# Clustered attention, an MLP and a soft mixture of experts in one kernel: the MLP stage's softmax in groups of two tiles, a fourth PSUM bank, tokens two chunks sooner

## The chip, the cores and the metric

The kernel runs on one core of a Trainium2 chip, as one program. The metric is the device time of one execution in microseconds. A core has five engines that run side by side, each through its own list of instructions in order, and that wait for one another by semaphores: TensorE (PE in the profile, with its weight loads as PEld), VectorE (DVE), ScalarE (ACT), GpSimd (POOL) and SyncE (SP), which here only issues DMA transfers. TensorE writes to PSUM, a small memory of eight banks; each bank holds 512 float32 numbers in each of 128 partitions.

## The reference

Three layers follow one another. Only the second and the logits and sums of the third lie in the stage that is changed.

```python
def _moe_ref(x, w_in, w_out):          # x: 3072 tokens x 512, from the attention
    h = x @ w_in                       # 512 -> 2048
    g = h * np.cos(h)
    return g @ w_out                   # 2048 -> 512

def _moe2_ref(x, phi, w1, w2):         # 32 slots, 8 experts
    logits = x @ phi
    d = np.exp(logits - logits.max(0)) ; d /= d.sum(0) + 1e-09     # softmax over all tokens
    slot_input = d.T @ x
    ...                                # each expert: relu(slot_input @ w1) @ w2
    c = np.exp(logits - logits.max(1)) ; c /= c.sum(1) + 1e-09     # softmax over the 32 slots
    return c @ slot_out
```

## The kernel before

The program has three stages: the attention, the MLP, and a tail with the experts and the output.

**The MLP stage** takes the 3072 tokens in 24 tiles of 128 tokens, and each tile in four chunks of 512 hidden columns: 96 chunks, numbered c, with c // 4 the tile for the first 22 tiles. (The last two tiles are taken together, chunk by chunk.) The loop at L1016 issues one chunk per pass, and every engine gets its instructions in the order in which the passes write them. No scheduler moves them. In pass c stand:

- `hchunk(c)`, L128: 12 matmuls of 512 columns that add up h in one PSUM bank with the tag "s". There are three such banks, so h of chunk c + 3 uses the bank of chunk c again.
- `post2(c-2)`, L855: ScalarE takes a sine, ScalarE or VectorE squares it, and VectorE writes g = h cos h (L865, called gg). This is the last reader of h, so it frees the bank.
- `post1(c-1)`, L139: a copy on ScalarE (L142), two operations on VectorE (L143, L144).
- `gtr(c-3)`, L867: four transposes of g on TensorE; `gev(c-4)`, L875: their copy out of PSUM into a buffer gts, of which there are four.
- In each fourth pass `logit` (L883): 4 matmuls per chunk, 16 in all, form the slot logits of a whole tile in the bank m1 (the trace shows each float32 matmul twice). wphi already holds w_out times phi, so that the logits come from g directly.
- Then the tile's online softmax, in steps that hang on one another over several passes. `soft1` (L901) copies the logits, `soft2` (L908) adds them up on TensorE into the bank m2 (lf, lt) and takes maxima on VectorE (L920 to L924). `softx` and `softe` (L928, L940) take exponentials on ScalarE; before them and behind them ScalarE loads another function table. `soft3` to `soft5` sum, transpose the exponentials (dt, bank v), multiply them with g (accp, bank v) and add the product to acc (L990).

A token tile comes in three steps: `xload` (L92, three DMAs on SP's queue into the one buffer xr), `xprep` (L103: GpSimd multiplies at L106, VectorE makes a mask at L108, GpSimd adds at L110) and `xprep2` (L112: VectorE casts the high part at L117, GpSimd makes the low part at L118, which is the last reader of xr). The table `xsched` (L1003) puts them in passes 4t - 5, 4t - 3 and 4t - 2 for tile t.

**The tail** multiplies with 32 MB of expert weights. They come in 16 pieces of 2 MB. Pieces 0 to 3 are loaded in passes 28, 36, 44 and 52 into buffers of the pool wk (six buffers; two hold w_out). Piece 4 follows when the last chunk with the first quarter of w_in is done (pass 89), as it takes that weight's place; pieces 5 to 7 follow in passes 91, 93 and 95, and the rest in the tail.

Of the kernel before, what the change touches and what calls it, by code (L numbers as in the profile page):

```python
# [8 lines left out]
F32 = mybir.dt.float32  # L9
# [10 lines left out]
P = 128  # L20
# [6 lines left out]
def clustered_attention_then_soft_moe(  # L27
# [16 lines left out]
    DM, DF = w_in.shape  # L44
    NS = phi.shape[1]
# [44 lines left out]
    R = {}  # L90
# [31 lines left out]
    order = [(t, f) for t in range(NT - GRP) for f in range(NF)]  # L122
    order += [(t, f) for f in range(NF) for t in range(NT - GRP, NT)]
    NC_ = len(order)
    groups = [[t] for t in range(NT - GRP)] + [list(range(NT - GRP, NT))]
    at_last = {max(c for c in range(NC_) if order[c][0] in ts): ts for ts in groups}

    def hchunk(c):  # L128
        t, f = order[c]
        hi, lo = R["xs", t]  # L130
        h = psum.tile([P, 512], F32, tag="s", name=f"h{c}", bufs=3)
        n = 0
        for d in range(DT):
            for x, w in ((hi, 0), (hi, 1), (lo, 0)):
                PE.matmul(h, lhsT=x[:, d, :], rhs=wc[f][:, w, d, :], start=(n == 0), stop=(n == 3 * DT - 1))  # L135
                n += 1
        R["h", c] = h
# [706 lines left out]
    with ExitStack() as m:  # L844
# [3 lines left out]
        R["m"] = m0  # L848
        zero = phis.rearrange("p a s -> p (a s)").bitcast(BF16)
        POOL.memset(zero, 0.0)  # L850
        wo = [wk.tile([P, 8, DM], F32, tag="wk", name=f"wo{x}") for x in range(2)]
        gs_stack = ExitStack()
        gsp = gs_stack.enter_context(tc.tile_pool(name="gsp", bufs=4))

        def post2(c):  # L855
            t, f = order[c]
            h, r = R.pop(("h", c)), R.pop(("r", c))
            if f == 0:
                R["g", t] = ggp.tile([P, DF], F32, tag="gg", name=f"gg{t}")
            ACT.activation(out=r, in_=r, func=AF.Sin, scale=0.5)  # L860
            if c == NC_ - 2 or (c % 4 in (0, 2)):
                ACT.activation(out=r, in_=r, func=AF.Square)  # L862
            else:
                (POOL if c == NC_ - 3 else DVE).tensor_tensor(out=r, in0=r, in1=r, op=ALU.mult)  # L864
            DVE.scalar_tensor_tensor(out=R["g", t][:, f * 512:(f + 1) * 512], in0=r, scalar=0.5, in1=h, op0=ALU.subtract, op1=ALU.mult)  # L865
# [7 lines left out]
            R["gp", c] = g  # L873

        def gev(c, eng=None):  # L875
            s = gsp.tile([P, 512], F32, tag="gts", name=f"gts{c}")
            if eng is DVE:
                DVE.tensor_copy(s, R.pop(("gp", c)))
            else:
                ACT.activation(out=s, in_=R.pop(("gp", c)), func=AF.Copy)  # L880
            R["gt", c] = s

        def logit(c):  # L883
            t, f = order[c]
            s = R.pop(("gt", c))
            if f == 0:
                if t < NT - GRP:
                    R["lp", t] = psum.tile([P, P], F32, tag="m1", name=f"lp{t}")
                elif t == NT - GRP:
                    R["lpg"] = psum.tile([P, GRP, P], F32, tag="m1", name="lpg")  # L890
                    for j in range(4):
                        PE.matmul(R["lpg"][32 * j:32 * j + 32].rearrange("p a b -> p (a b)"), lhsT=zero[:, 0:32], rhs=zero,
                                  start=True, stop=False)
                if t >= NT - GRP:
                    R["lp", t] = R["lpg"][:, t - NT + GRP, :]
            lp = R["lp", t]
            for j in range(4):
                PE.matmul(lp[32 * j:32 * j + 32, :], lhsT=wphi[:, 4 * f + j, :], rhs=s[:, j * P:(j + 1) * P],  # L898
                          start=(f == 0 and t < NT - GRP), stop=(f == NF - 1 and (t < NT - GRP or t == NT - 1)))
# [8 lines left out]
        def soft2(ts):  # L908
            n = len(ts)
            lps = R["lps"]  # L910
            lfb = psum.tile([P, n * (P + NS)], F32, tag="m2", name=f"lf{ts[0]}")
            lf = lfb[:, 0:n * P]
            lt = lfb[:, n * P:].rearrange("p (a b) -> p a b", a=n)
            PE.matmul(lf, lhsT=gflat, rhs=lps, start=True, stop=True)
            for y in range(n):
                PE.matmul(lt[:, y, :], lhsT=lps[:, y * P:(y + 1) * P], rhs=gmat[:, 0, :], start=True, stop=True)
            mn = mp.tile([P, 1], F32, tag="mrun", name=f"mrun{ts[0]}")
            ng = mp.tile([P, 1], F32, tag="ng", name=f"ng{ts[0]}")
            rn = mp.tile([P, n], F32, tag="rn", name=f"rn{ts[0]}")
            DVE.tensor_reduce(out=mn, in_=lf, op=ALU.max, axis=AX.X)  # L920
            DVE.tensor_tensor(out=mn, in0=mn, in1=R["m"], op=ALU.max)
            DVE.tensor_scalar(out=ng, in0=mn, scalar1=-1.0, scalar2=None, op0=ALU.mult)
            DVE.tensor_reduce(out=rn, in_=lt, op=ALU.max, axis=AX.X)
            DVE.tensor_scalar(out=rn, in0=rn, scalar1=-1.0, scalar2=None, op0=ALU.mult)  # L924
            R["soft2"] = lf, lt, R["m"], ng, rn
            R["m"] = mn
# [47 lines left out]
        def soft4(ts):  # L974
            n = len(ts)
            cr, dts = R["dts"]
            ap = psum.tile([P, 512], F32, tag="v", name=f"accp{ts[0]}")
            for y, t in enumerate(ts):
                g = R.pop(("g", t))
                for j in range(4):  # L980
                    PE.matmul(ap[32 * j:32 * j + 32, :], lhsT=dts[:, y * P + 32 * j:y * P + 32 * j + 32],  # L981
                              rhs=g[:, j * 512:(j + 1) * 512], start=(y == 0), stop=(y == n - 1))
            R["ap"] = cr, ap
# [18 lines left out]

        xsched = {}  # L1003
        for t in range(1, NT):
            c0 = min(4 * t - 5, NF * (NT - GRP) - 4 - 3 * (NT - 1 - t))
            for fn, dc in ((xload, 0), (xprep, 2), (xprep2, 3)):
                if c0 + dc >= 2:
                    xsched.setdefault(c0 + dc, []).append((fn, t))
# [6 lines left out]

        for c in range(2, NC_):  # L1016
            hchunk(c)
            post2(c - 2)
            if c - 1 < NC_ - 1:
                post1(c - 1)  # L1020
            if c >= 4:
                gev(c - 4)
            if c - 6 in at_last:
                softx(at_last[c - 6])
                softe(at_last[c - 6])
            if c - 7 in at_last and at_last[c - 7][0] != NT - GRP - 1:
                soft3(at_last[c - 7])
            for fn, t in xsched.get(c, ()):
                fn(t)
            late_c = at_last.get(c - 7)  # L1030
            if late_c and late_c[0] == NT - GRP - 2:
                soft3b(late_c)
            if c >= 3:
                gtr(c - 3)
            if c % 4 == 3:
                for x in range(max(c - 7, 0), c - 3):
                    logit(x)
            if c - 4 in at_last:
                soft1(at_last[c - 4])
            if c - 5 in at_last:  # L1040
                soft2(at_last[c - 5])
            if late_c and late_c[0] < NT - GRP - 2:
                soft3b(late_c)
            elif late_c and late_c[0] == NT - GRP - 2:
                soft4(late_c)
                soft5(late_c)
            if at_last.get(c - 6) == [NT - GRP - 1]:
                soft3b(at_last[c - 6])
                soft3(at_last[c - 6])
            elif at_last.get(c - 7) == [NT - GRP - 1]:  # L1050
                soft4(at_last[c - 7])
            late_c = at_last.get(c - 8)
            if late_c and late_c[0] < NT - GRP - 2:
                soft4(late_c)
                soft5(late_c)
            if c == 5:
                recip(B - 1)
                while late:
                    tick()
            if c in (12, 20):  # L1060
                x = (c - 12) // 8
                for y in range(2):
                    SP.dma_start(out=wo[x][:, 4 * y:4 * y + 4], in_=wod.rearrange("(f y p) d -> y p f d", f=4, p=P)[2 * x + y])
            if c in (28, 36, 44, 52):
                load_piece((c - 28) // 8, wk, "wk")
            if c == NC_ - 6:
                w8 = R["mxa"].tile([P, 1024], F32, tag="xr", name="w8b", bufs=1)
                load_part(8, 2, w8)
            if NC_ - GRP * NF <= c and (NC_ - 1 - c) % GRP == 0:
                if c == NC_ - 1:  # L1070
                    w8 = ggp.tile([P, 2, 1024], F32, tag="gg", name="w8a")
                    for e in range(2):
                        load_part(8, e, w8[:, e])
                load_piece(NF - 1 - (NC_ - 1 - c) // GRP + 4, wbig, "wbig")
# [248 lines left out]
```

## Time and profile before

| | us |
|---|---|
| three runs | 905.78, 907.83, 907.93 (median 907.83) |
| the profiled execution, its own time | 906.36 |
| its span in the profile | 904.6 |

| engine | busy us | share of the span |
|---|---|---|
| PE | 873.0 | 97% |
| PEld (weight loads) | 623.2 | 69% |
| DVE | 702.2 | 78% |
| ACT | 666.4 | 74% |
| POOL | 453.0 | 50% |

The MLP stage's first h matmul starts at 452.7 us and its last one starts at 833.3 us. Before it lies the attention, behind it the tail. In a row of the timeline, the first number is the start in microseconds from the span's start, the second the time that the merged instructions took; then come engine, source line, operation, what is written from what, the shapes and the count. A bracket at the end tells how long the engine sat idle before it and which instruction ended that. Matmuls overlap, so the step from one row's start to the next one's tells more of TensorE's pace than a row's length.

### The profile page before, as it was taken

To read this page: it belongs to the slowest core of one execution; us is meant where nothing else is said; L and a number is where in the kernel's file an instruction comes from. 1 tells how busy PE (TensorE), PEld (TensorE's weight loads), DVE (VectorE), ACT (ScalarE), POOL (GpSimd) and SP (SyncE) were. 2 spreads that over 40 slices of the span, in tenths; PEclk is the share of its full clock that TensorE was granted. 3 is DMA by queue.
4 is the path that set the end of the run, shared out by engine and by line. 5 is a ranking of instruction groups with operands and counts; after the bars stand their busy time and mean duration, and the time that the engine had idled before them with its cause. 6 is when DMAs were issued, how large, how long until landed. Compare 5 with 4: busy or idle time off the path is not lost.

```text
span 904.6 us, 16891 instructions
## 1 busy us (share of the span) xinstructions
PE 873.0 (97%) x5991; PEld 623.2 (69%) x5991; DVE 702.2 (78%) x1495; ACT 666.4 (74%) x1364; POOL 453.0 (50%) x344
## 2 busy tenths in 40 slices
PE   7899999999999999999999999999999999999996
PEld 4666767676667676666567777777777777777443
DVE  7899898988899889999967777777777767776203
ACT  6688888898888898886556676777767777676323
POOL 3478888888788887889832222222322222310000
PEclk9999999999999999999999999999999999999998
DMA  7676766765766675644310431333040101128998
GB/s 165 143 180 165 192 164 160 181 164 145 190 159 170 171 183 142 176 132 142 111 34 26 140 117 48 117 128 126 27 141 24 47 25 40 32 76 301 392 351 301
DMA packets 127816, 129.51 MB, mean 143 GB/s; under 512 B 57851, under 2 KB 105205, under 8 KB 127733
## 3 DMA queue, kind: packets, MB, share of 16 engines
q1 hardware_dynamic: 126020, 128.02, 49.2%
q8 instruction: 47, 0.77, 0.4%
q10 hardware_dynamic: 1712, 0.43, 0.2%
q14 instruction: 37, 0.29, 0.1%
HBM read 86.18 MB, written 16.97 MB: 114 GB/s over the span
## 4 chain that ended last, share of the span: by engine, by line
PE 33%; DVE 5%; ACT 5%; issue 4%; DMA 2%; SPq 2%; POOL 1%; POOLq 0%; ACTq 0%
PE h L135 21%; PE gt L872 3%; PE lp L898 2%; SPq L836 2%; PE accp L981 2%; DMA wh<-in_moe_w_dram 2%; DVE gg L865 1%; PE fo L1257 1%; ACT L860 1%; ACT kk L860 1%; ACT L936 1%; DVE kk L144 1%; ACT kk L862 1%; PE o L453 1%; DVE kk L864 1%
## 5 line engine op out<-in xcount | busy, mean ns | idle before, releaser
L471 POOL TENSOR_TENSOR ps<-ps,a 128x768 f32<-128x768 f32 x124 | 233.9, 1886 | 60.4 <-ACT a L444 55.4
L135 PE MATMUL h<-wc,xhi 128*128 128x512 f32 x768 | 251.5, 408 | 5.3 <-DVE gg L865 5.2
L396 DVE TENSOR_REDUCE mc<-sm 128x1 f32<-128x384 f32 x384 | 200.2, 553 | 33.7 <-PE sm L394 30.3
L444 ACT ACTIVATE a<-s 128x384 f32<-128x384 f32 x384 | 179.4, 494 | 19.4 <-PE s L441 13.7
L135 PEld LDWEIGHTS h<-wc,xhi 128*128 128x128 f32 x768 | 137.7, 189 | 55.0 <-DVE kk L144 16.8
L135 PE MATMUL h<-wc,xlo 128*128 128x512 f32 x384 | 152.5, 397 | 0.0
L440 PE MATMUL s<-st 96*128 96x384 f32 (+1 forms) x384 | 142.9, 372 | 1.3 <-ACT a L444 0.2
L453 PE MATMUL o<-a,vt 128*64 128x384 f32 x768 | 136.0, 497 | 0.0
L441 PE MATMUL s<-st 128*128 128x384 f32 x384 | 131.1, 341 | 0.0
L394 PE MATMUL sm<-st 96*128 96x384 f32 x384 | 123.2, 356 | 4.8 <-DVE mc L396 3.4
L865 DVE SCALAR_TENSOR_TENSOR gg<-kk,h 128x512 f32<-128x512 f32 x96 | 66.0, 688 | 51.7 <-ACT kk L862 48.3
L453 PEld LDWEIGHTS o<-a,vt 128*64 128x64 f32 x768 | 53.0, 138 | 64.9 <-issue 60.7
L860 ACT ACTIVATE kk<-kk 128x512 f32<-128x512 f32 x96 | 60.7, 632 | 40.1 <-DVE kk L144 39.8
L440 PEld LDWEIGHTS s<-st 96*128 96x128 f32 (+1 forms) x384 | 73.1, 190 | 23.9 <-issue 17.5
L135 PEld LDWEIGHTS h<-wc,xlo 128*128 128x128 f32 x384 | 72.5, 189 | 17.6
L106 POOL TENSOR_TENSOR xr<-xr 128x512 f32<-128x512 f32 x24 | 31.2, 1301 | 105.6 <-DMA xr<-recs 105.6
L394 PEld LDWEIGHTS sm<-st 96*128 96x128 f32 x384 | 72.0, 191 | 13.8 <-DVE mc L396 6.9
L441 PEld LDWEIGHTS s<-st 128*128 128x128 f32 x384 | 73.0, 190 | 0.0
L110 POOL TENSOR_TENSOR xr<-xr 128x512 f32<-128x512 f32 x24 | 31.3, 1306 | 80.3 <-DVE xr L108 76.0
L118 POOL TENSOR_TENSOR xlo<-xr,xhi 128x512 fp32r<-128x512 f32 x24 | 36.5, 1521 | 67.3 <-DVE xhi L117 67.3
L144 DVE SCALAR_TENSOR_TENSOR kk<-kk,h 128x512 f32<-128x512 f32 x96 | 66.0, 688 | 3.3
L468 POOL TENSOR_TENSOR ps<-a,a 128x768 f32<-128x768 f32 x31 | 56.8, 1833 | 6.9 <-ACT a L444 4.9
(230 smaller groups left out, 1495.4 us busy)
## 6 DMA issues: line engine op xcount, KB each, us to landing
st<-st SPq DMA_DIRECT2D x128, 192.0 KB
w<-in_moe_w_dram SPq DMA_DIRECT2D x8, 2048.0 KB
wh<-in_moe_w_dram SPq DMA_DIRECT2D x23, 512.0 KB
w<-in_moe_w_out_dram SPq DMA_DIRECT2D x16, 512.0 KB
w<-in_moe_w_in_dram SPq DMA_DIRECT2D x16, 512.0 KB
qt<-in_q_dram SPq DMA_DIRECT2D x32, 192.0 KB
vt<-in_v_dram SPq DMA_DIRECT2D x16, 384.0 KB
xnum<-num SPq DMA_DIRECT2D x32, 192.0 KB
```

The lines of the kernel that those rows point to most:

```text
L135: PE.matmul(h, lhsT=x[:, d, :], rhs=wc[f][:, w, d, :], start=(n == 0), stop=(n == 3 * DT - 1))
L144: DVE.scalar_tensor_tensor(out=a, in0=a, scalar=-TWO_PI, in1=h, op0=ALU.mult, op1=ALU.add)
L394: PE.matmul(m[:, 0:QW], lhsT=st[0:96, Q1 + h, qt * P:(qt + 1) * P], rhs=st[0:96, K1 + h, half * QW:(half + 1) * QW], start=True, stop=True)
L396: DVE.tensor_reduce(out=s["mc"][:, col:col + 1], in_=m[:, 0:QW], op=ALU.max, axis=AX.X)
L440: PE.matmul(x[:, 0:QW], lhsT=st[0:n, K1 + h, ks], rhs=st[0:n, Q1 + h, qs], start=True, stop=False)
L441: PE.matmul(x[:, 0:QW], lhsT=st[:, K2 + h, ks], rhs=st[:, Q2 + h, qs], start=False, stop=True)
L444: ACT.activation(out=T[i][u][:, h, :], in_=x[:, 0:QW], func=AF.Exp, scale=scale)
L453: PE.matmul(s["o"][64 * h:64 * h + 64, 0:QW], lhsT=s["v"][:, h, kt, :], rhs=t[:, h, :], start=(kt == 0), stop=(kt == KT - 1))
L468: (DVE if i == NPAIR - 1 and qc else POOL).tensor_tensor(out=ps, in0=s[u - 1], in1=t, op=ALU.add)
L471: (DVE if i == NPAIR - 1 and qc else POOL).tensor_tensor(out=ps, in0=ps, in1=t, op=ALU.add)
L860: ACT.activation(out=r, in_=r, func=AF.Sin, scale=0.5)
L865: DVE.scalar_tensor_tensor(out=R["g", t][:, f * 512:(f + 1) * 512], in0=r, scalar=0.5, in1=h, op0=ALU.subtract, op1=ALU.mult)
```

## The change

The softmax of tiles 0 to 19 is done for two tiles at a time. The logits of eight chunks (32 matmuls) run in one pass, c % 8 == 3; the two tiles share one logit bank, one copy, one sum, one set of maxima, one table load to the exponentials and one back. The products with g follow 12 passes behind the pair's last chunk instead of 8 behind the tile's. Tiles 20 to 23 stay as they are.

Since g of five tiles must now be kept, two more slots (gx) and the eight gts slots (gtx) are taken from the pool wk. The sum lf moves from bank m2 to m1, which it shares with the logits, and each fourth chunk's h goes to m2. Token loads, preparation and split stand two passes sooner (4t - 7, 4t - 5, 4t - 4; tile 2 one pass). Weight pieces 2 and 3 take the buffers of gtx and gx, and so move from passes 44 and 52 to passes 84 and 88.

```diff
-    groups = [[t] for t in range(NT - GRP)] + [list(range(NT - GRP, NT))]
+    NPR = 20
+    groups = [[t, t + 1] for t in range(0, NPR, 2)] + [[t] for t in range(NPR, NT - GRP)] + [list(range(NT - GRP, NT))]
...
     def hchunk(c):
         t, f = order[c]
         hi, lo = R["xs", t]
-        h = psum.tile([P, 512], F32, tag="s", name=f"h{c}", bufs=3)
+        if c % 4 == 3:
+            h = psum.tile([P, 512], F32, tag="m2", name=f"h{c}")
+        else:
+            h = psum.tile([P, 512], F32, tag="s", name=f"h{c}", bufs=3)
...
+        gtx = wk.tile([P, 8, 512], F32, tag="wk", name="gtx")
+        gx = wk.tile([P, 2, DF], F32, tag="wk", name="gx")
...
-                R["g", t] = ggp.tile([P, DF], F32, tag="gg", name=f"gg{t}")
+                if t < NPR and t % 5 > 2:
+                    R["g", t] = gx[:, t % 5 - 3]
+                else:
+                    R["g", t] = ggp.tile([P, DF], F32, tag="gg", name=f"gg{t}")
...
-            s = gsp.tile([P, 512], F32, tag="gts", name=f"gts{c}")
+            s = gtx[:, c % 8] if c < NF * NPR else gsp.tile([P, 512], F32, tag="gts", name=f"gts{c}")
...
-                if t < NT - GRP:
+                if t < NPR:
+                    if t % 2 == 0:
+                        R["lpg"] = psum.tile([P, 2, P], F32, tag="m1", name=f"lp{t}")
+                    R["lp", t] = R["lpg"][:, t % 2, :]
+                elif t < NT - GRP:
                     R["lp", t] = psum.tile([P, P], F32, tag="m1", name=f"lp{t}")
...
-            lfb = psum.tile([P, n * (P + NS)], F32, tag="m2", name=f"lf{ts[0]}")
+            lfb = psum.tile([P, n * (P + NS)], F32, tag="m1", name=f"lf{ts[0]}")
...
-            c0 = min(4 * t - 5, NF * (NT - GRP) - 4 - 3 * (NT - 1 - t))
+            c0 = min(max(4 * t - 7, 3 * t - 4), NF * (NT - GRP) - 4 - 3 * (NT - 1 - t))
...
-            if c % 4 == 3:
-                for x in range(max(c - 7, 0), c - 3):
+            if c < NF * (NPR + 1):
+                if c % 8 == 3:
+                    for x in range(max(c - 11, 0), c - 3):
+                        logit(x)
+            elif c % 4 == 3:
+                for x in range(c - 7, c - 3):
                     logit(x)
...
+            late_c = at_last.get(c - 12)
+            if late_c and late_c[0] < NPR - 2:
+                soft4(late_c)
+                soft5(late_c)
             late_c = at_last.get(c - 8)
-            if late_c and late_c[0] < NT - GRP - 2:
+            if late_c and NPR - 2 <= late_c[0] < NT - GRP - 2:
                 soft4(late_c)
                 soft5(late_c)
...
-            if c in (28, 36, 44, 52):
-                load_piece((c - 28) // 8, wk, "wk")
+            if c in (28, 36, 84, 88):
+                load_piece((28, 36, 84, 88).index(c), wk, "wk")
```

Three places show how the instructions move. The first is TensorE's list around the logits of tile 10 (lp10); gt are transposes, accp the products with g, lf the sums, x4 counts matmuls of one form. Before, and then in the changed kernel:

```order
L872 MATMUL gt44_8239<-ident_68,gg11_8186 128x128 x4
L898 MATMUL lp10_8244<-gts40_8112,wphi_78 32x128 x4
L898 MATMUL lp10_8244<-gts41_8152,wphi_78 32x128 x4
L898 MATMUL lp10_8244<-gts42_8194,wphi_78 32x128 x4
L898 MATMUL lp10_8244<-gts43_8233,wphi_78 32x128 x4
L981 MATMUL accp9_8263<-gg9_7834,dts9_8211 32x512 x4
...
L872 MATMUL gt45_8291<-ident_68,gg11_8186 128x128 x4
L914 MATMUL lf10_8296<-lps10_8261,gmat_74 128x128
L916 MATMUL lf10_8296<-gmat_74,lps10_8261 128x32
```

```order
L881 MATMUL gt48_8172<-ident_68,gg12_8131 128x128 x4
L911 MATMUL lp10_8177<-gtx_6305,wphi_78 32x128 x32
L994 MATMUL accp8_8212<-gx_6306,dts8_8024 32x512 x8
...
L881 MATMUL gt49_8247<-ident_68,gg12_8131 128x128 x4
L927 MATMUL lf10_8252<-lps10_8210,gmat_74 128x256
L929 MATMUL lf10_8252<-gmat_74,lps10_8210 128x32 x2
```

Two tiles' logits and two tiles' products now stand in one block, the sum is one matmul of 256 columns, and it comes four chunks later (behind gt49 instead of gt45).

The second place is VectorE's list around the maxima of tile 10 (mrun10, ng10, rn10); the cast xhi belongs to a later tile. Before, and then in the changed kernel:

```order
L117 CAST xhi12_8200<-xr12_8058 128x512
L864 TENSOR_TENSOR kk45_8190<-kk45_8190 128x512
L865 SCALAR_TENSOR_TENSOR gg11_8186<-kk45_8190,h45_8132 128x512
L143 TENSOR_SCALAR kk46_8229<-kk46_8229 128x512
L144 SCALAR_TENSOR_TENSOR kk46_8229<-kk46_8229,h46_8173 128x512
L990 SCALAR_TENSOR_TENSOR acc_6297<-acc_6297,corr9_8154,accp9_8263 128x512
...
L144 SCALAR_TENSOR_TENSOR kk47_8285<-kk47_8285,h47_8213 128x512
L920 TENSOR_REDUCE mrun10_8299<-lf10_8296 128x1
L921 TENSOR_TENSOR mrun10_8299<-mrun10_8299,mrun9_8122 128x1
L922 TENSOR_SCALAR ng10_8300<-mrun10_8299 128x1
```

```order
L1003 SCALAR_TENSOR_TENSOR acc_6297<-acc_6297,corr8_7971,accp8_8212 128x512
L874 SCALAR_TENSOR_TENSOR gg12_8131<-kk50_8161,h50_8118 128x512
L147 TENSOR_SCALAR kk51_8238<-kk51_8238 128x512
L148 SCALAR_TENSOR_TENSOR kk51_8238<-kk51_8238,h51_8145 128x512
L117 CAST xhi14_8243<-xr14_8109 128x512
L933 TENSOR_REDUCE mrun10_8256<-lf10_8252 128x1
L934 TENSOR_TENSOR mrun10_8256<-mrun10_8256,mrun8_7942 128x1
L935 TENSOR_SCALAR ng10_8257<-mrun10_8256 128x1
```

The cast, and with it the GpSimd operation that follows it, has moved to a place right ahead of the maxima.

The third place is SP's list behind the last token loads (w2 to w7 are weight pieces). Before, and then in the changed kernel:

```order
L97 DMA xr23_9878<-xnum3_83 128x4x128
L100 DMA xr23_9878<-recs3_91 64x4x128 x2
L841 DMA w4_10104<-in_moe2_w1_dram 128x4x1024
L836 DMA w8b_10148<-in_moe2_w2_dram 128x1024
L841 DMA w5_10197<-in_moe2_w1_dram 128x4x1024
```

```order
L97 DMA xr23_9500<-xnum3_83 128x4x128
L100 DMA xr23_9500<-recs3_91 64x4x128 x2
L845 DMA w2_9521<-in_moe2_w1_dram 128x4x1024
L845 DMA w3_9701<-in_moe2_w1_dram 128x4x1024
L845 DMA w4_9738<-in_moe2_w1_dram 128x4x1024
L840 DMA w8b_9782<-in_moe2_w2_dram 128x1024
L845 DMA w5_9831<-in_moe2_w1_dram 128x4x1024
```

Pieces 2 and 3 now stand between the last token load and piece 4.

## Rows read from the trace of the kernel before

**Rows 1.** Windows, mid stage: stretch, length, five engines busy (PE first), clock, DMA share, GB/s.

```profile
526.30:651.70 125.40, 125.38 (x875) 97.73 (x873) 94.26 (x233) 93.45 (x185) 33.43 (x24) 1.00 0.31 102
```

**Rows 2.** Waits view of PE and PEld, 452 to 836 us.

```profile
PE h L135 <- DVE gg L865: 5.2, 7, 2.0
...
PEld h L135 <- DVE gg L865: 7.6, 9, 2.3
```

**Rows 3.** Timeline and windows around the longest of these waits.

```profile
772.95 0.88 DVE L108 TENSOR_SCALAR xr<-xr,vm 128x128 f32<-128x128 f32 x4 [2.52 <-POOL xr L106]
...
777.11 1.22 PE L135 MATMUL h<-wc,xhi 128*128 128x512 f32 x2 [2.04 <-DVE gg L865]
...
778.00:779.00 1.00, 1.00 (x4) 0.71 (x4) 0.45 (x2) 1.00 (x1) 0.40 (x1) 0.50 0.00 0
...
781.57 0.60 PE L872 MATMUL gt<-ident,gg 128*128 128x128 f32 x4
```

**Rows 4.** Timeline of PE, one tile (four chunks) without a wait.

```profile
620.40 0.73 PE L135 MATMUL h<-wc,xhi 128*128 128x512 f32 x2
...
623.30 0.60 PE L872 MATMUL gt<-ident,gg 128*128 128x128 f32 x4
...
625.70 0.73 PE L135 MATMUL h<-wc,xhi 128*128 128x512 f32 x2
...
628.60 0.60 PE L872 MATMUL gt<-ident,gg 128*128 128x128 f32 x4
629.03 0.39 PE L914 MATMUL lf<-lps,gmat 128*128 128x128 f32 x2
629.26 0.31 PE L916 MATMUL lf<-gmat,lps 128*128 128x32 f32 x2
629.40 0.71 PE L135 MATMUL h<-wc,xhi 128*128 128x512 f32 x2
...
632.28 0.60 PE L872 MATMUL gt<-ident,gg 128*128 128x128 f32 x4
632.63 0.72 PE L135 MATMUL h<-wc,xhi 128*128 128x512 f32 x2
...
636.04 0.74 PE L135 MATMUL h<-wc,xhi 128*128 128x512 f32 x2
```

**Rows 5.** Timeline, a tile's softmax on ACT, then the DVE and PE instructions behind it.

```profile
756.98 1.28 ACT L936 ACT_TABLE_LOAD   x1 [0.51 <-DVE rn L923]
...
758.81 0.28 ACT L944 ACTIVATE e<-lf,rn 128x32 f32<-128x32 f32 x1
...
759.20 1.28 ACT L860 ACT_TABLE_LOAD   x1
...
761.83 0.69 DVE L865 SCALAR_TENSOR_TENSOR gg<-kk,h 128x512 f32<-128x512 f32 x1 [1.57 <-ACT kk L862]
...
762.57 0.73 PE L135 MATMUL h<-wc,xhi 128*128 128x512 f32 x2
```

**Rows 6.** Timeline, the small maximum at L921 alone, and beside a GpSimd operation.

```profile
756.45 0.16 DVE L921 TENSOR_TENSOR mrun<-mrun,mrun 128x1 f32<-128x1 f32 x1
...
773.97 1.27 POOL L110 TENSOR_TENSOR xr<-xr 128x512 f32<-128x512 f32 x1 [1.05 <-DVE xr L108]
774.06 1.20 DVE L921 TENSOR_TENSOR mrun<-mrun,mrun 128x1 f32<-128x1 f32 x1
```

**Rows 7.** DMA issues of the page; timeline and windows at the stage's end.

```profile
w<-in_moe_w_dram SPq DMA_DIRECT2D x8, 2048.0 KB
...
809.76 0.38 SPq L841 DMA_DIRECT2D w<-in_moe_w_dram  x1
...
825.00:830.00 5.00, 5.00 (x29) 3.81 (x32) 2.57 (x8) 4.85 (x12) 0.00 (x0) 1.00 0.55 186
830.00:835.00 5.00, 5.00 (x60) 3.57 (x52) 3.11 (x7) 2.80 (x6) 1.04 (x1) 1.00 1.02 360
```

**Rows 8.** Timeline of POOL, the first token operation behind a 2 MB piece.

```profile
568.80 1.29 POOL L106 TENSOR_TENSOR xr<-xr 128x512 f32<-128x512 f32 x1 [7.24 <-DMA xr<-recs]
```

## The prediction

> **What bounds the kernel now.** I read the busy lines of the page first: TensorE has 97% of the span. The windows view tells whether that is real work. In the middle of the MLP stage TensorE is busy in 125.38 of 125.40 us, at the full clock of 2.4 GHz (column PEclk 1.00), and no other engine comes near [rows 1]. So in this stage time is saved in two ways only: TensorE waits less, or it gets less to do.
>
> The waits view of the stage comes next. TensorE waits for one thing: the operation gg at L865, which frees an h bank. The weight loads, which are what TensorE does first in a chunk, waited 7.6 us for it, 9 times, at most 2.3 us; the matmuls behind them show 5.2 us in 7 waits [rows 2]. I count the weight loads' figure, since a chunk can't begin without them.
>
> The timeline at the longest wait shows a second cost. VectorE stood 2.52 us for the tokens of a tile whose load came late, gg slid back, and TensorE stood still. From then its granted clock was 0.50, its lower level of 1.2 GHz, and that chunk took 781.57 - 777.11 = 4.46 us [rows 3] where an undisturbed one takes 623.30 - 620.40 = 2.90 us [rows 4]. So 1.56 us more belong to this wait.
>
> Last I read how near the other tiles are to waiting. After a tile's softmax on ScalarE, gg starts at 761.83, ends 0.69 later at 762.52, and the h chunk that needs its bank starts at 762.57 [rows 5]. The slack is 0.05 us. Nothing may be added to that path with three banks.
>
> **The change part by part.** The sum is made against the profiled execution's own 906.36 us (span 904.6, the 1.8 around it left alone). The median of the runs is 1.5 us above that; the runs spread over 2.15 us, more than the differences that I expect between single tiles, and I forecast on the scale of the profile.
>
> *Fourth bank.* h of chunk c + 4, not c + 3, now needs gg of chunk c. The transposes of chunk c need it too, and they stand behind h of chunk c + 3. So the relief is one chunk of h matmuls, 2.90 us [rows 4], and the longest wait was 2.3 [rows 2]. All nine go, if nothing else comes later: -7.6. What is late next is looked at below. I leave one ninth in place, +0.8, for the first tiles, whose tokens can't come sooner: tile 2's load waits for tile 1's split in the one buffer xr. Ends: nothing left, or half left (+3.8).
>
> *Tokens two passes sooner.* The same three GpSimd operations, five VectorE ones and three DMAs per tile, two passes ahead on VectorE's and POOL's lists and on SP's queue. Each load still waits for the split before it, so in the steady tiles only the place moves. The longest wait is different: there a cap put tile 21's load into the pass of tile 20's split. Now the load stands one pass behind it. With the wait goes the low clock: -1.56. Tile 23 keeps such a pass.
>
> *Less for TensorE.* Two tiles have the same number of logit matmuls and products, and as these stream back to back (2.40 us from 623.30 to 625.70 [rows 4]) I count no gain. The sum lf is another matter. A chunk with it takes 629.40 - 628.60 = 0.80 us from its transposes to the next h, one without 632.63 - 632.28 = 0.35: lf and lt cost 0.45 per tile. For a pair, the second lt costs 629.40 - 629.26 = 0.14, and 128 more columns in two matmuls cost 2 x 128/512 of an h matmul, itself about 2.90/12 = 0.24: 0.12. So 0.71 instead of 0.90, 0.19 per pair, 10 pairs: -1.9. Ends: 0, and -4.5 if the second tile's share were free.
>
> *Less for ScalarE and VectorE.* Half the softmax steps of 20 tiles go, among them 20 table loads of 1.28 us [rows 5]. Neither bounds the stage, so this counts as slack and not as time.
>
> *The pair's own path.* It is longer than a tile's, and with 0.05 us of slack this is what could turn the sign. Logits of eight chunks and two products stand ahead on TensorE itself, so they delay both sides alike. From the sum on, the other side grows. The second e adds 759.20 - 758.81 = 0.39 [rows 5]. At the most everything between the table loads doubles (758.26 to 759.20: 0.94), and the maxima too (756.45 to 756.98: 0.53 [rows 5, 6]): 1.47. Then the collision. Alone the maximum at L921 takes 0.16; beside a GpSimd addition it took 1.20 [rows 6]. In the changed list the cast stands right ahead of the maxima and GpSimd's subtraction follows the cast, so each pair may meet it: 1.04 more. Together 0.4 to 2.5 us against 0.05 + 2.90 = 2.95. I take it as covered: 0. With three banks the same pairs would wait.
>
> The Trainium skill (SBUF — State Buffer, Who interferes with whom) says that a VectorE operation with two inputs in SBUF and a GpSimd operation that reads SBUF share a port, and that the second blocks until the first ends. The trace agrees: 1.20 against 0.16. By that rule the collision is no accident but comes with every pair; by the rows it costs TensorE nothing while the bank's relief holds.
>
> *Weight pieces 2 and 3 in passes 84 and 88.* The tail is where the transfers bound: from 830 us on the DMA engines are full (share 1.02, 360 GB/s). Before that they are not: 0.55 at 186 GB/s from 825 to 830, which is 338 GB/s while busy, and 2.25 us idle [rows 7]. A piece is 2.1 MB [rows 7], 6.2 us at that rate. Piece 2 goes out behind tile 23's load, about five chunks ahead of piece 4, and has the engines to itself. Piece 3 waits for the products of tiles 18 and 19 in pass 87. On SP, piece 4 and all behind it stand behind this wait. From those products to the end of chunk 89, which releases piece 4 (809.76 before [rows 7]), lie two chunks: 2 x (2.90 + 0.35) + 0.45 = 6.95 us. So piece 3 is through when piece 4 may start, and a spill up to 2.25 us falls into the idle time. I take 0; ends 0 and 12.4, both pieces in full.
>
> Sum: 906.36 - 7.6 - 1.56 - 1.9 + 0.8 = 896.1. I say 896.
>
> **The rivals.**
>
> *Waits stay in part.* Piece 2 stands right behind tile 23's load. The one row like that shows GpSimd waiting 7.24 us for its tokens [rows 8], and tile 23 has its split and load so close that VectorE may again stand, as it did for 2.52. If that gives one long wait and its low clock back, 2.3 + 1.56, the time is 900. Against it: the fourth bank covers 2.9.
> The Trainium skill (DMA: Bandwidth & Descriptors, Issuing engines are not separate DMA queues) says that transfers run on the same 16 engines and interleave. The 7.24 us agree with that.
>
> *One piece spills into the tail.* If piece 3 comes a piece late, the full tail shifts by 6.2: 902. For it: the tail has no idle time after 830. Against it: the 6.95 us.
>
> *Gain and loss cancel.* Both pieces spill (+12.4, 908.5), or the collision isn't covered and each pair waits 1.04 (+10.4, 906.5).
>
> *Slower: the pair's path outgrows the bank.* Place: gg of the chunks behind a pair's table loads. VectorE also stands at L1003 for two products, with gg of the next chunk behind it, and then has the cast, the collision and the maxima in a row. If the path is 2.3 us over, as long as the worst wait before, ten pairs cost 23: 919. It decides from 1.0 us per pair, where it eats the gain of 10.3. For it speaks the 0.05 us; against it that even the upper bound of 2.5 lies under 2.95.
>
> **How the numbers follow.** Forecast 896: 0.64. Waits stay in part, 900: 0.16. One piece spills, 902: 0.08. Gain and loss cancel, 906.5 to 908.5: 0.07. Slower, 919: 0.05. What a measurement can tell from no change is 0.3%, 2.7 us around 907.83. So faster 0.88, the same 0.07, slower 0.05. The range reaches from 891 (no wait left, lf almost free: 906.36 - 9.16 - 4.5 = 892.7, less the 1.5 us by which the runs lie on either side) to 904, which takes in the second and third case. About 0.13 lies outside.
>
> **What would show it.** Right: in the profile after, the waits view has hardly a wait of PE or PEld for gg; the granted clock is 1.00 throughout the stage; two tiles take about 31.1 us (2 x 15.64 - 0.19; a tile is 636.04 - 620.40 [rows 4]); from the first h to the last the stage is some 10 us shorter; from piece 4's issue to the end it is as long as before, 904.6 - 809.76 = 94.8 us [rows 7]. Wrong: a wait of h or gt for gg in every second tile at the same chunk means the pair's path; a tail longer than 95 us with the DMA share at 1.0 from piece 3 on means the pieces; VectorE waiting at the mask of tile 23 means the late load.

## The result, and the profile after

The changed kernel takes 897.39 us (median of four runs, 896.75 to 897.91) against 906.81 us for the kernel before (905.68 to 907.93). The ratio is 0.9887, 95% interval 0.9872 to 0.9902: 1.1% faster. The profiled execution took 897.9 us, and its span is 896.2 us against 904.6.

The stage is where the time went. From the start of the first h to the start of the last, TensorE took 833.31 - 452.72 = 380.59 us before and 824.69 - 454.21 = 370.47 us now: 10.1 us less. The span is only 8.4 us shorter, because in this execution the first h starts 1.5 us later. That lies in the attention, which is untouched; in a second profile of the same kernel the first h starts at 452.80, the stage is again 370.47 and the span 894.9.

In mid stage TensorE still never rests, at the full clock (windows view of the changed kernel, columns as in [rows 1]):

```profile
526.30:651.70 125.40, 125.40 (x914) 99.14 (x916) 90.61 (x201) 80.93 (x160) 32.79 (x25) 1.00 0.26 84
```

ScalarE has 12.5 us less to do there, but TensorE was the bound in [rows 1], and it still is. What it does in one pair shows in its timeline, start us, duration, operation:

```profile
554.67 0.71 PE L139 MATMUL h<-wc,xhi 128*128 128x512 f32 x2
...
557.56 0.60 PE L881 MATMUL gt<-ident,gg 128*128 128x128 f32 x4
558.09 1.95 PE L911 MATMUL lp<-gtx,wphi 128*32 128x128 f32 x64
559.86 1.04 PE L994 MATMUL accp<-gg,dts 128*32 128x512 f32 x8
560.72 1.04 PE L994 MATMUL accp<-gx,dts 128*32 128x512 f32 x8
561.69 0.73 PE L139 MATMUL h<-wc,xhi 128*128 128x512 f32 x2
...
564.60 0.60 PE L881 MATMUL gt<-ident,gg 128*128 128x128 f32 x4
565.03 0.60 PE L927 MATMUL lf<-lps,gmat 128*128 128x256 f32 x2
565.46 0.53 PE L929 MATMUL lf<-gmat,lps 128*128 128x32 f32 x4
565.83 0.72 PE L139 MATMUL h<-wc,xhi 128*128 128x512 f32 x2
...
585.49 0.71 PE L139 MATMUL h<-wc,xhi 128*128 128x512 f32 x2
```

The pair takes 585.49 - 554.67 = 30.82 us; two tiles took 2 x 15.64 = 31.28 [rows 4]. One block of 64 logit matmuls and 16 products, from transposes to h, is 561.69 - 557.56 = 4.13. Before there were two blocks of 625.70 - 623.30 = 2.40 [rows 4], so 0.67 is gone; part of it comes back, since a chunk that had such a block now has a plain gap of about 0.35 from its transposes to h. The sum lf is no cheaper than before: 565.83 - 564.60 = 1.23, less that gap 0.88, where two tiles paid 0.90.

The waits view of the stage shows what is left where [rows 2] had 5.2 and 7.6 us:

```profile
PE gt L881 <- DVE gg L874: 1.8, 2, 1.5
PE gt L881 <- ACT gts L889: 1.3, 1, 1.3
...
PE gt L881 <- ACT gtx L889: 0.2, 1, 0.2
```

No h waits for gg any more. The 1.8 us are waits of the transposes, while the third tile's h is running. Chunk by chunk, against the same chunk of a steady pair, the first five tiles lose 0.2 to 1.6 us at six places, 3.4 us in all. The timelines of POOL, DVE and PE at the worst of them answer to [rows 3]:

```profile
485.96 1.29 POOL L106 TENSOR_TENSOR xr<-xr 128x512 f32<-128x512 f32 x1 [4.63 <-DMA xr<-recs]
...
487.29 0.88 DVE L108 TENSOR_SCALAR xr<-xr,vm 128x128 f32<-128x128 f32 x4 [1.46 <-POOL xr L106]
...
491.07 1.30 POOL L118 TENSOR_TENSOR xlo<-xr,xhi 128x512 fp32r<-128x512 f32 x1 [1.49 <-DVE xhi L117]
...
491.29 1.63 DVE L873 TENSOR_TENSOR kk<-kk 128x512 f32<-128x512 f32 x1 [0.36 <-ACT kk L869]
492.95 0.69 DVE L874 SCALAR_TENSOR_TENSOR gg<-kk,h 128x512 f32<-128x512 f32 x1
...
493.79 0.63 PE L881 MATMUL gt<-ident,gg 128*128 128x128 f32 x4 [1.45 <-DVE gg L874]
```

It is tile 21's pattern in small: VectorE stands at the mask for tokens (1.46 us), then its square L873 meets GpSimd's subtraction L118 (1.63 us where the square alone takes 0.68), and gg is late. The granted clock stays at 1.00 from 484 to 500 us.

### The profile page after: what moved, and what is told of

Same layout as the page of the kernel before. It is cut to its first block, busy times and chain, and to the rows that moved or that the text cites. A ratio compares the mean times of both kernels' runs of the same rounds, so it can differ in the third digit from the quotient of the medians.

```text
span 896.2 us, 16761 instructions
## 1 busy us (share of the span) xinstructions
PE 867.8 (97%) x5971; PEld 621.9 (69%) x5971; DVE 685.5 (76%) x1405; ACT 631.3 (70%) x1294; POOL 448.2 (50%) x344
## 4 chain that ended last, share of the span: by engine, by line
PE 38%; issue 4%; DVE 3%; SPq 2%; DMA 2%; ACT 1%; POOL 1%; POOLq 0%; ACTq 0%
PE h L139 25%; PE gt L881 4%; PE lp L911 2%; PE accp L994 2%; SPq L840 2%; PE fo L1278 1%; DMA wh<-in_moe_w_dram 1%; DMA xr<-recs 1%; PE o L457 1%; PE so L1254 1%; PE lf L927 0%; DVE kk L148 0%; DVE gg L874 0%; POOL xlo L118 0%; PE lf L929 0%
## 5 line engine op out<-in xcount | busy, mean ns | idle before, releaser
L139 PE MATMUL h<-wc,xhi 128*128 128x512 f32 x768 | 248.8, 405 | 0.0
L874 DVE SCALAR_TENSOR_TENSOR gg<-kk,h 128x512 f32<-128x512 f32 x64 | 43.9, 686 | 45.4 <-ACT kk L871 42.6
L146 ACT ACTIVATE kk<-h 128x512 f32<-128x512 f32 x96 | 55.9, 582 | 1.1 <-PE h L139 1.0
```

Source lines behind the costliest of these rows:

```text
L146: ACT.activation(out=a, in_=h, func=AF.Copy, scale=1.0 / TWO_PI)
```

## The experiments

All runs are compared with the kernel before, on the same chip. The stage is counted from the first h to the last in each profile; a pair is two steady tiles.

| kernel | median us | ratio, 95% interval | stage us | pair us |
|---|---|---|---|---|
| before | 906.81 to 908.15 | 1 | 380.59 | 31.30 |
| changed | 897.39 | 0.9887 [0.9872, 0.9902] | 370.47 | 30.81 |
| e2 fourth bank alone | 902.94 | 0.9942 [0.9925, 0.9959] | 375.20 | 31.17 |
| e5 sooner tokens alone | 904.22 | 0.9955 [0.9941, 0.9970] | 376.97 | 31.29 |
| e7 bank and tokens | 902.62 | 0.9949 [0.9936, 0.9961] | 374.04 | 31.17 |
| e4 late pieces alone | 907.06 | 0.9992 [0.9983, 1.0001] | 378.94 | 31.29 |
| e3 changed, three banks | 912.02 | 1.0048 [1.0029, 1.0066] | 385.52 | 32.15 |
| e1 changed, old token passes | 903.32 | 0.9953 [0.9936, 0.9969] | 376.68 | 31.56 |
| e6 changed, tiles 2 and 3 later, tile 1 twice | 898.82 | 0.9904 [0.9891, 0.9918] | 372.26 | 30.81 |
| e8 changed, tiles 2 to 4 later | 897.72 | 0.9891 [0.9878, 0.9905] | 371.00 | 30.81 |
| e9 changed, tiles 2 and 3 later | 897.51 | 0.9879 [0.9860, 0.9897] | 370.86 | 30.81 |
| e10 changed, again | 897.48 | 0.9883 [0.9866, 0.9900] | 370.47 | 30.81 |

**e2: the fourth bank alone**, in the kernel before.

```diff
+        if c % 4 == 3:
+            h = psum.tile([P, 512], F32, tag="m2", name=f"h{c}")
+        else:
+            h = psum.tile([P, 512], F32, tag="s", name=f"h{c}", bufs=3)
-            lfb = psum.tile([P, n * (P + NS)], F32, tag="m2", ...
+            lfb = psum.tile([P, n * (P + NS)], F32, tag="m1", ...
```

> The kernel before with the fourth bank alone (lf in m1, every fourth h in m2). Theory A (the bank takes the waits for gg, the pairs take 0.4 to 0.5 us of TensorE work each): all waits of before but some tenths go, 906.8 - 8.8 - 0.8 = 897 to 899; a tile takes 15.6 us still. Rival B (a single tile's logits and sum in one bank m1 make TensorE or ScalarE wait for each other): waits of lp for the exponentials appear in each tile and the time is 903 or more.

The stage lost 5.4 us. No matmul of h waits for gg any more, but the waits view names other operations (first three lines), and the timeline of DVE at tile 21 shows what is behind one of them, the 0.8 us that lp loses there:

```profile
PE lp L901 <- ACT gts L883: 1.8, 3, 1.0
PE gt L875 <- ACT gts L883: 1.7, 2, 1.3
PE accp L984 <- ACT dts L974: 1.5, 1, 1.5
```

```profile
767.62 0.87 DVE L108 TENSOR_SCALAR xr<-xr,vm 128x128 f32<-128x128 f32 x4 [1.56 <-POOL xr L106]
768.41 0.28 DVE L923 TENSOR_REDUCE mrun<-lf 128x1 f32<-128x128 f32 x1
768.73 1.22 DVE L924 TENSOR_TENSOR mrun<-mrun,mrun 128x1 f32<-128x1 f32 x1
```

VectorE still stands for tile 21's tokens. The maxima behind it are late, so ScalarE's exponentials and table loads are late, and the copies queued behind these on ScalarE are what the logits now wait for. The bank removes the wait for a bank; the delay itself goes on by another way. Neither guess holds: the 897 to 899 of theory A isn't reached, and rival B's wait in each tile isn't there either, since a pair of tiles takes 31.17 us.

**e5: the sooner tokens alone.**

```diff
-            c0 = min(4 * t - 5, NF * (NT - GRP) - ...
+            c0 = min(max(4 * t - 7, 3 * t - 4), NF * (NT - GRP) - ...
```

> The kernel before with the token steps two passes sooner alone. Theory A (sooner tokens make VectorE stand in the first tiles, and with three banks each such stand reaches TensorE): the first tiles lose 3 to 6 us, the late wait at tile 21 (2.3 us and 1.6 us of clock) goes, in sum 906 to 910. Rival B (they take waits away and add none): 902 to 903.

The stage lost 3.6 us, and the time lies between the two guesses. In its trace the waits at tiles 6 to 21 are gone, the one at tile 21 with its low clock included; those of the first tiles are 1.7 us larger than before, start to start (VectorE's mask comes too early there), less than theory A's 3 to 6. What is left in the waits view of PEld, beside the 7.6 of [rows 2]:

```profile
PEld h L135 <- DVE gg L865: 5.4, 6, 1.5
```

**e7: bank and tokens, without the pairs.**

> The kernel before with the fourth bank and the sooner tokens, one tile per softmax and the pieces where they were. Theory (bank and tokens take the waits together, pairs only shorten TensorE's work): two steady tiles take 31.17 us, as with the bank alone, against 30.81 with pairs, so ten pairs are worth 3.6 and the time is 900 to 902, with no wait at tile 21. Rival (pairs also take waits away, because half of ScalarE's table loads go): waits on ScalarE's copies in lp, gt and accp stay as in the run with the bank alone, and the time is 902 to 904.

The stage is 374.04, 3.57 longer than with pairs, and the pair of tiles takes 31.17 against 30.81: ten times 0.36 is 3.6. The early waits are about as large as in the changed kernel (3.6 and 3.4 us). So this is what the pairs are worth on top of the bank and the tokens (pairs alone were not run). The time, 902.62, lies just over the theory's 900 to 902 and within the rival's; the trace decides for the theory, since behind the third tile there is no more waiting than with pairs.

```profile
PE lp L901 <- ACT gts L883: 2.0, 2, 1.0
PE gt L875 <- ACT gts L883: 1.8, 3, 1.3
```

These are chunks 7 and 11, and 1.3 us in gt at the very end of the stage, which the changed kernel has too.

**e3: the changed kernel with three banks.**

```diff
-        if c % 4 == 3:
-            h = psum.tile([P, 512], F32, tag="m2", name=f"h{c}")
-        else:
-            h = psum.tile([P, 512], F32, tag="s", name=f"h{c}", bufs=3)
+        h = psum.tile([P, 512], F32, tag="s", name=f"h{c}", bufs=3)
```

(and lf back in m2.)

> The changed kernel with three h banks (lf back in m2, all h in the tag s). Theory A (the pair's path is 0.4 to 2.5 us longer than a tile's, and the tile's had 0.05 us of slack): h waits for gg once in each pair, 0.4 to 2.5 us, 10 pairs, so 901 to 922, likely 907; the wait stands at the h chunk behind dt. Rival B (pairs need no bank, as the second tile of a pair has no softmax and gives slack back): no such wait, 898 to 899.

Slower than before. In each pair h waits twice for gg, where theory A had one wait: 0.5 us behind the table loads and 0.8 us behind the cast; the pair takes 32.15. The waits view, and the second of these places in the timelines of DVE and PE:

```profile
PE h L136 <- DVE gg L871: 8.5, 16, 1.4
PE h L136 <- DVE gx L871: 3.5, 8, 0.6
```

```profile
618.14 1.62 DVE L870 TENSOR_TENSOR kk<-kk 128x512 f32<-128x512 f32 x1 [0.36 <-ACT kk L866]
619.79 0.69 DVE L871 SCALAR_TENSOR_TENSOR gx<-kk,h 128x512 f32<-128x512 f32 x1
```

```profile
620.54 0.73 PE L136 MATMUL h<-wc,xhi 128*128 128x512 f32 x2 [0.54 <-DVE gx L871]
```

So the rival "the pair's path outgrows the bank" is real where the bank is missing: it is the bank that lets the pairs pay.

**e1: the changed kernel with the old token passes** (the line of e5, reversed).

> The changed kernel with the token steps back in passes 4t-5, 4t-3, 4t-2; everything else stays. Theory A (the sooner tokens cost time in the first tiles, because VectorE then stands at the mask for a load that can't come sooner): the waits of gt for gg at chunks 9 and 10 and the small ones before them, 3.7 us in all, fall under 1 us, and the time is 894 to 895. Rival B (the sooner tokens are a part of the gain, since they take away the wait for tile 21's tokens): that wait comes back, up to 2.3 us and 1.6 us of low clock, the time is 898 to 901.

The time rose by 6, and the place is one that I had not named. The waits at chunks 7, 9 and 10 went, though around chunk 16 tile 4 lost 1.4 us more than later tiles do, and no wait came back at tile 21. But in each pair h of the even tile waits about 0.75 us for the low part of its own tokens. The waits view, then DVE, POOL and PE at one of these places:

```profile
PE h L139 <- POOL xlo L118: 5.3, 10, 1.0
```

```profile
605.33 0.42 DVE L117 CAST xhi<-xr 128x512 fp32r<-128x512 f32 x1
```

```profile
605.90 1.60 POOL L118 TENSOR_TENSOR xlo<-xr,xhi 128x512 fp32r<-128x512 f32 x1 [3.56 <-DVE xhi L117]
```

```profile
607.55 0.50 PE L139 MATMUL h<-wc,xlo 128*128 128x512 f32 x1 [0.49 <-POOL xlo L118]
```

In the old pass the cast stands on VectorE behind gg and the pair's softmax steps, which wait for ScalarE's two table loads; it reaches GpSimd at 605.90, and h of the next tile has already begun. With pairs the sooner tokens are not only a cure for tile 21: each pair needs them.

**e4: only the two weight pieces later**, in the kernel before.

```diff
-            if c in (28, 36, 44, 52):
-                load_piece((c - 28) // 8, wk, "wk")
+            if c in (28, 36, 84, 88):
+                load_piece((28, 36, 84, 88).index(c), wk, "wk")
```

> The kernel before with weight pieces 2 and 3 issued in passes 84 and 88 and nothing else changed. Theory (the prediction's): each transfer has the engines to itself for five chunks and a spill fits the idle time, so 0: within 1.5 us of before, 906 to 909, and from piece 4's issue to the end as long as before. Rival: one piece spills into the full tail, +6 us, 913 to 914; or both, +12 us, 919 to 920. What hides in the trace of the changed kernel is whether this cost was paid and covered by other gains.

No difference beyond the interval. Piece 4 goes out at 809.09, and 904.1 - 809.09 = 95.0 us later the span ends; before it was 94.8. The test is milder than the changed kernel, since nothing holds the buffers of pieces 2 and 3 here: both go out by 793.40, some 16 us ahead of piece 4. The stage is 1.65 shorter in this profile. At the late tokens of tile 21 TensorE waited 1.67 us for gg instead of 2.04, and its granted clock stayed at 1.00 where it had been 0.50 [rows 3]; but the next h then waited too, which it had not done before:

```profile
777.21 0.73 PE L135 MATMUL h<-wc,xhi 128*128 128x512 f32 x2 [1.67 <-DVE gg L865]
...
781.32 0.73 PE L135 MATMUL h<-wc,xhi 128*128 128x512 f32 x2 [0.49 <-DVE gg L865]
```

```profile
778.00:780.00 2.00, 2.00 (x10) 1.61 (x9) 0.56 (x2) 1.96 (x3) 1.30 (x1) 1.00 0.00 0
```

The two chunks around this place took 782.03 - 771.58 = 10.45 us before and 781.32 - 772.06 = 9.26 now: 1.2 less, 0.4 of it a shorter wait and 0.8 the clock. The rest of the 1.65 are smaller waits at tiles 13 and 14.

**e6: the tokens of tiles 2 and 3 one pass later**, to remove the 3.4 us.

```diff
-            c0 = min(max(4 * t - 7, 3 * t - 4), ...
+            c0 = min(max(4 * t - 7, 3 * t - 3), ...
```

> The changed kernel with the tokens of tiles 2 and 3 one pass later (max(4t-7, 3t-3)): loads in passes 3, 6, 9, 13 instead of 2, 5, 9, 13. Theory: the 3.7 us that TensorE still waits in the first five tiles come from VectorE standing at the mask for tokens that are asked for too early; half or more goes, 895 to 896. Rival: VectorE stands at the next tile's mask instead, and the time stays at 896.5 to 898.

The edit also moved tile 1, whose first step is written ahead of the loop, so that its tokens were prepared twice and the output is wrong. TensorE lost 4.6 us by this around the start of tile 1, with a granted clock of 0.57 (mean from 470 to 474 us) behind the wait, and only 0.5 us of the other early waits were left. The run doesn't answer the question; e9 does.

**e8 and e9: tiles 2 to 4 later; tiles 2 and 3 later and tile 1 left alone.**

```diff
# e8
+            c0 = min(max(4 * t - 7, min(4 * t - 5, 3 * t - 2)), ...
# e9
+            c0 = min(max(4 * t - 7, 3 * t - 4 + (t > 1)), ...
```

> The changed kernel with the tokens of tiles 2 to 4 later still: loads in passes 3, 7, 10, 13 instead of 2, 5, 9, 13. Theory: the early waits go as they did in the run with the old token passes, where the first three tiles had none, and the other tiles keep their sooner tokens: 893.5 to 895. Rival: h of tile 4 or 5 waits for its lower part, as with the old passes, and the time is 896 to 898.

> The changed kernel with the tokens of tiles 2 and 3 one pass later (loads in passes 3, 6, 9, 13 instead of 2, 5, 9, 13) and tile 1 left where it is; in the run e6_tiles_2_3_later tile 1's tokens were also prepared a second time, by a slip of the edit, so its output wasn't the reference's and h of tile 1 waited 4.4 us. Theory: without that, hardly a wait is left in the first five tiles (that run had 0.5 us behind chunk 4), so 3.2 us less than the changed kernel: 893.5 to 895. Rival: with tile 1 on time the waits come back at the chunks of tile 2, as in the changed kernel and in the run with tiles 3 and 4 later: 896 to 898.

> The changed kernel as it is, on the same chip as e9_tiles_2_3_once, so that the two can be compared: 897.4 within 1 us, the waits of 3.7 us at chunks 4 to 10 again in its trace. Rival: those waits were an accident of one execution, and the trace has them elsewhere or not at all.

My theory fell in both. The early waits moved and kept their sum: in e9 h of tile 2 waits 0.87 for its low part, and 2.9 more come at chunks 11 to 19, where VectorE now stands for tile 4's tokens instead of tile 3's (timeline of DVE, e9):

```profile
499.64 0.88 DVE L108 TENSOR_SCALAR xr<-xr,vm 128x128 f32<-128x128 f32 x4 [2.56 <-POOL xr L106]
```

The changed kernel, run again, had its waits at the same chunks as the first time (0.40, 0.32, 1.63 us at chunks 7, 9 and 10), so they are no accident. e9 and e10 ran on one chip and can't be told apart, 897.51 and 897.48. No version here beats the changed kernel. One buffer xr serves all tiles, and each load waits for the split before it; a second buffer wasn't tried.

## Why the prediction was right, and where its steps were off

The forecast of 896 and its sign hold, but two terms were mis-sized, in opposite directions: 2.6 us too little was left in place, and 3.0 too little was taken from TensorE's work. That the sum is met within a few tenths is in part luck.

*Fourth bank, -7.6.* The nine waits of h are gone, as predicted; from start to start they were 7.1 us, since a part of the weight loads' idle time lies under matmuls that still run. That the bank takes them alone is wrong: e2 gained 5.4 us of stage, not 7.6 + 1.56, because 4.8 us came back, at chunks 4, 7, 11, 83, 87 and 90, nearly all as waits for ScalarE's copies. Bank and tokens overlap: 5.4 and 3.6 alone, 6.55 together (380.59 - 374.04). *What is left, 0.8.* Mis-sized: 3.4 us. I had the place and the reason (the single buffer xr), but took a ninth of the waits; the transposes gt need gg as well, and the first tiles' tokens come so early that VectorE stands in front of it. e6, e8 and e9 show that this can be moved and not how it can be removed.

*Tokens and low clock, -1.56.* Right in this pair of profiles: the granted clock is 1.00 in the whole stage. But e4 has the wait of tile 21 and not the low clock, so the low clock need not come with this wait; and without it the next h waited 0.49, so that the clock alone cost 0.8 there and not 1.56. "Two passes sooner" is also not true of the last tiles: the cap leaves tile 21 one pass sooner, and tiles 22 and 23 where they were.

*Less for TensorE, -1.9.* Mis-sized: 10 x 0.49 = 4.9. The pairs bring 3.6 (e7 against the changed kernel), but not by lf, which costs 0.88 against 0.90. They bring it by the logits and products, for which I had counted no gain because the matmuls stream back to back. A block has a beginning and an end: the first h behind the products starts 0.52 us after the start of the last of them, and behind transposes 0.03 after that of the last. One block fewer per pair saves this 0.49; the longer block gives 0.18 of it back (64 logit matmuls and 16 products), and lf brings 0.03. This is read from the rows; no run changes the blocks alone.

The other 1.3 (0.13 in each pair of tiles) come with the bank: e2 has 31.17 against 31.30 with it, and 31.29 without it (e5). They were small waits in steady tiles, below what the waits view lists. The slack of 0.05 us that I read in [rows 5] was none. The gg that ended the longest wait ended at 776.37 + 0.69 = 777.06, and h started at 777.11 [rows 3]; e3's h at 620.54 starts 0.06 behind its gg after a wait of 0.54. So 0.05 is how far h starts behind a gg that it has waited for, and the h of [rows 5] was waiting as well: it starts 0.09 us after dt (0.08 in most tiles), where with the fourth bank h follows dt by 0.03. That makes some 0.1 of the 0.13 in two tiles. From before, DVE at the longest wait and PE in [rows 5]:

```profile
776.37 0.69 DVE L865 SCALAR_TENSOR_TENSOR gg<-kk,h 128x512 f32<-128x512 f32 x1
```

```profile
762.48 0.27 PE L969 MATMUL dt<-ident,d 128*128 128x128 f32 x1
```

*The pair's own path, 0.* Right with the fourth bank. The timelines of DVE, POOL and PE in the changed kernel, at the two late places of a pair:

```profile
566.49 0.16 DVE L934 TENSOR_TENSOR mrun<-mrun,mrun 128x1 f32<-128x1 f32 x1
...
572.27 0.69 DVE L874 SCALAR_TENSOR_TENSOR gg<-kk,h 128x512 f32<-128x512 f32 x1 [2.72 <-ACT kk L871]
...
580.93 1.29 POOL L118 TENSOR_TENSOR xlo<-xr,xhi 128x512 fp32r<-128x512 f32 x1 [1.49 <-DVE xhi L117]
...
581.15 1.62 DVE L873 TENSOR_TENSOR kk<-kk 128x512 f32<-128x512 f32 x1 [0.36 <-ACT kk L869]
582.80 0.69 DVE L874 SCALAR_TENSOR_TENSOR gg<-kk,h 128x512 f32<-128x512 f32 x1
```

```profile
575.41 0.60 PE L881 MATMUL gt<-ident,gg 128*128 128x128 f32 x4
...
585.13 0.60 PE L881 MATMUL gt<-ident,gg 128*128 128x128 f32 x4
```

Behind the table loads gg ends at 572.96, 2.45 us before its transposes. The collision is real but stands elsewhere: the maximum (L934) takes 0.16, as alone in [rows 6], and it is the square L873 that takes 1.62 beside GpSimd's low part of the other tile. There gg ends at 583.49, 1.64 us before its transposes. With three banks the h one chunk sooner, at 582.25, would have had to wait 1.24 for it; e3 shows 0.8 there, since its first wait had already set TensorE back by 0.5. The Trainium skill (SBUF — State Buffer, Who interferes with whom) says that the second of two such operations blocks until the first ends. The trace agrees: the operation ends at 582.77, 0.55 us after GpSimd's (580.93 + 1.29 = 582.22), somewhat less than the 0.68 that it takes alone.

*Late pieces, 0.* Right, in e4 and, under the tighter order, in the changed kernel, where SP issues pieces 2, 3 and 4 at 783.44, 794.49 and 801.14:

```profile
783.44 0.55 SPq L845 DMA_DIRECT2D w<-in_moe_w_dram  x1
...
794.49 0.38 SPq L845 DMA_DIRECT2D w<-in_moe_w_dram  x1
...
801.14 0.37 SPq L845 DMA_DIRECT2D w<-in_moe_w_dram  x1
```

From piece 4 to the end are 896.2 - 801.14 = 95.1 us, against 94.8 [rows 7]. Piece 3 has 6.65 us, close to the 6.95 worked out, and that is just enough: the share of the DMA engines is 1.06 up to 801 us and falls to 0.20 in the microsecond in which piece 4 goes out (windows view, columns as in [rows 1]).

```profile
800.00:801.00 1.00, 1.00 (x6) 0.76 (x5) 0.97 (x3) 0.99 (x5) 0.00 (x0) 1.00 1.06 438
801.00:802.00 1.00, 1.00 (x8) 0.90 (x7) 0.61 (x1) 0.98 (x4) 0.00 (x0) 1.00 0.20 78
```

*The rivals.* Tile 23 doesn't wait: its load goes out ahead of piece 2 (781.70 against 783.44), GpSimd has the tokens after the usual 4.46 us, and VectorE's mask at 790.45 follows without idle time. No piece spills. Gain and loss did cancel in part, but between terms that I had at 0.8 and 1.9, not where that rival put it.

Sum from the traces: -7.1 (waits of h, start to start) - 1.6 (clock) - 4.9 + 3.4 = -10.2; measured -10.1. Predicted for the stage: -10.3. On the profile's own scale the forecast is met too: 897.9, less the 1.5 by which the first h came late, is 896.4.

## What to carry to other kernels

A resource that frees a wait (a bank) and a schedule that avoids its cause (tokens sooner) overlap; price them together, and ask which engine's queue carries the delay on once the first wait is gone. When work is grouped, count the beginnings and ends of the blocks, not only the instructions: here they were worth some 3 us, with as many logit matmuls and products as before. And an edit that looks like an extra (the fourth bank for the pairs, the sooner tokens for the pairs) may be what makes the main one pay: without either, 6 to 15 us were lost.

## What the runs showed of the hardware that was not expected

TensorE's granted clock fell to its lower level of 1.2 GHz after a wait of 2.04 us in one execution (0.50), and in e6 behind a wait of 2.68 us (0.57 as the mean of 4 us); in e4, after 1.67 us at the same place, it stayed at 1.00. A wait that shrinks a little can therefore give back more than itself: in this pair of executions 0.4 us less waiting came with 1.55 us less of slow matmuls in the chunk behind it (4.46 to 2.91), of which 0.8 was left after the next h had waited for its gg.
